# Gated linear attention and a cosine-gated feed-forward on one core: inputs of three batches loaded whole, four state updates dropped, another order

## The chip, the cores and the metric

The kernel runs on one core of a Trainium2 chip. The metric is the device time of one execution, in microseconds (us). Of the kernel before, two timed runs are shown, 201.43 and 202.99, with a median of 202.21. A third execution was recorded by the hardware profiler; its own time is 200.76, and from its first to its last instruction (the span) it took 198.7.

The core has five instruction streams that run side by side. TensorE (PE, with its weight loads as PEld) multiplies matrices and transposes. VectorE (DVE) and ScalarE (ACT) empty PE's results. GpSimd (POOL) prepares operands. SyncE (SP) issues all DMAs here. Each stream does its instructions in the order in which they were written, and waits for what it needs from the others.

## The reference

Per batch (4) and head (8), a gated recurrence runs over 768 positions with rows of 48 numbers. Its output, with the heads side by side, goes through a feed-forward layer of 384 to 2048 to 384.

```python
for t in range(S):                                   # B, H, S, D = 4, 8, 768, 48
    state = alpha[:, :, t, :, None] * state + einsum('bhd,bhe->bhde', k[:, :, t], v[:, :, t])
    y[:, :, t] = einsum('bhd,bhde->bhe', q[:, :, t], state)
x = y.transpose(0, 2, 1, 3).reshape(B * S, H * D)    # 3072 x 384
h = x @ w_in                                         # 384 x 2048
out = (h * cos(h)) @ w_out                           # 2048 x 384
```

The state starts at zero in each batch.

## The kernel before

The 768 positions of a batch are cut into six chunks of 128, so there are 24 chunks, numbered 0 to 23; chunks 0, 6, 12 and 18 are the first of their batch. All work on a chunk is cut into units, each a few instructions, and one long string (ORDER, lines 373 to 401) names the units in the order in which they are to be written into the instruction streams. A unit is a letter with a chunk's number. The scheduling is by hand: the string alone decides in which order each engine does its work.

Loading and preparing a chunk:

- `a`, `k`, `q`, `v` load one chunk's rows of alpha, k, q and v (192 KB each, lines 94 to 103). The rows of eight heads lie far apart in memory, and each row of 48 floats is 192 bytes long. `a` has four buffers of two chunks; the others have six of one chunk each.
- `l` (or `i` for one chunk) takes the logarithm of two chunks' alpha on ACT (line 142). `C` (or `c`) sums it along the positions on PE (lines 155, 159). `E` (or `d`) makes the cumulated product and its inverse with two exponentials on ACT (lines 173, 175).
- `K` and `Q` scale k and q by them on POOL (lines 183, 189; `Q` of chunks 0 and 1 on DVE). `b` casts v to bf16 on POOL (line 193). `E_` makes the mask with which the state is scaled (line 198).

The recurrence within a chunk:

- `T` transposes k and q (line 211, eight transposes), and `t` copies them out on DVE.
- `A` forms the scores (line 228), and `m` masks them on DVE (line 237).
- `S` is the chunk's addition to the state (line 250, four matmuls), and `u` adds and scales the state (line 262 on DVE, line 264 on POOL). The state after the last chunk of a batch is read by nobody, yet it is computed.
- `Y` forms the output (lines 279, 282), `y` casts it (line 289), `D` transposes it (line 298), and `B` copies that out on DVE (line 303).

The feed-forward of a chunk, in two halves:

- `F` and `G` multiply by w_in (line 315, 24 matmuls each). `f_` and `g_` take the cosine on ACT (line 323), and `p` and `Q_` multiply by it on DVE (line 329).
- `V` and `W` multiply by w_out (line 337, eight matmuls each). `e` copies the result out on ACT and stores it (lines 342, 343).

The weights are loaded in four quarters each, 768 KB per DMA: `z0` to `z3` for w_in, `Z0` to `Z3` for w_out (lines 109, 122). They are cast to bf16 by `r` on DVE and `s` on ACT for w_in, and by `R` for w_out (even quarters on DVE, odd quarters on ACT). The float32 copies have tiles of their own, w1f and w2f, so a load never waits for a cast. `F` needs quarters 0 and 1 of w_in, `G` needs 2 and 3; `V` needs quarters 0 and 1 of w_out, and `W` needs 2 and 3.

`w` followed by a number writes that many matmuls on zeros (line 353). Their result is not used; they keep PE occupied. The string holds 69 of them, all written ahead of `F2`.

PE's results lie in three kinds of buffers: "big" (three buffers: `C`/`c`, `A`, `F`, `G` take turns), "g" (one buffer: `T`, `S`, `Y` and `D` take turns, each after the one before has been copied out), and "o" (one buffer, `V` and `W`). DMAs have eight semaphores in turn, so that each DMA is issued only after the one eight before it has landed; SP issues them in the string's order, stores among them.

Of the kernel before, what the change touches and what calls it, by code (L numbers as in the profile page):

```python
# [9 lines left out]
FP = mybir.dt.float32  # L10
# [6 lines left out]
def kernel(  # L17
# [17 lines left out]
    NF = DF // C  # L35
    HF = NF // 2
    HD = H * D
    CW = HD + NP
    ACOL = [(h % 2) * NP + h // 2 for h in range(H)]
    PF = 6  # L40

    consts = ctx.enter_context(tc.tile_pool(name="consts", bufs=1))
    apool = ctx.enter_context(tc.tile_pool(name="apool", bufs=4))
    inpool = ctx.enter_context(tc.tile_pool(name="inpool", bufs=PF))
    cpool = ctx.enter_context(tc.tile_pool(name="cpool", bufs=4))
    work = ctx.enter_context(tc.tile_pool(name="work", bufs=2))
    moe = ctx.enter_context(tc.tile_pool(name="moe", bufs=2))
    ps = ctx.enter_context(tc.tile_pool(name="ps", bufs=1, space=bass.MemoryType.PSUM))
# [31 lines left out]
    nc.vector.memset(m2[0:64, 0:1], 1.0)  # L80
    nc.vector.memset(m2[64:128, 1:2], 1.0)

    w1f = consts.tile([C, 3, DF], FP, tag="w1f")
    w1 = consts.tile([C, 3, DF], BF, tag="w1")
    w2f = consts.tile([C, NF, DM], FP, tag="w2f")
    w2 = consts.tile([C, NF, DM], BF, tag="w2")

    a_t, q_t, k_t, v_t, cp_t, icp_t = {}, {}, {}, {}, {}, {}

    def rows(t, j):  # L90
        b, c = j // NC, j % NC
        return t[b, :, c * C : (c + 1) * C, :].rearrange("h s d -> s h d")

    def load_a(j):
        if j % 2 == 0:
            a_new = apool.tile([C, 2, H, D], FP, tag="a_sb")
            a_t[j // 2] = a_new
        nc.sync.dma_start(out=a_t[j // 2][:, j % 2], in_=rows(alpha, j))  # L98

    def load(nm, src, d, j):  # L100
        t = inpool.tile([C, H, D], FP, tag=nm)
        nc.sync.dma_start(out=t, in_=rows(src, j))  # L102
        d[j] = t

    QF = DF // 4

    def load_w1(h):
        f = slice(h * QF, (h + 1) * QF)
        nc.sync.dma_start(out=w1f[:, :, f], in_=moe_w_in[:, f].rearrange("(k p) f -> p k f", p=C))

    def cast(eng, dst, src):
        if eng is nc.scalar:
# [3 lines left out]

    def cast_w1(h, eng, k0, k1):
        f = slice(h * QF, (h + 1) * QF)
        cast(eng, w1[:, k0:k1, f], w1f[:, k0:k1, f])

    def load_w2(h):
        nc.sync.dma_start(
            out=w2f[:, 4 * h : 4 * h + 4],
            in_=moe_w_out[4 * h * C : (4 * h + 4) * C, :].rearrange("(f p) n -> p f n", p=C),
        )

    def cast_w2(h):
        cast((nc.vector, nc.scalar)[h % 2], w2[:, 4 * h : 4 * h + 4], w2f[:, 4 * h : 4 * h + 4])


    table = [None]
# [6 lines left out]
    def ln(j0, n):  # L138
        lnset()
        g = j0 // 2  # L140
        lo = j0 % 2
        nc.scalar.activation(  # L142
            out=lnab[:, g % 2, lo : lo + n, :, 0:D], in_=a_t[g][:, lo : lo + n], func=AF.Ln
        )

    cum_ps = {}
# [33 lines left out]

    def khat(j):
        icp = icp_t[j // 2][:, j % 2]
        nc.gpsimd.tensor_tensor(out=khb[:, j % 3, :, 0:D], in0=k_t.pop(j),  # L183
                                in1=icp.rearrange("s (h d) -> s h d", h=H), op=ALU.mult)

    def qhat(j):
        cp = cp_t[j // 2][:, j % 2]
        eng = nc.vector if j < 2 else nc.gpsimd
        eng.tensor_tensor(out=qhb[:, j % 3, :, 0:D], in0=q_t.pop(j),  # L189
                          in1=cp[:, 0:HD].rearrange("s (h d) -> s h d", h=H), op=ALU.mult)  # L190

    def vcast(j):
        nc.gpsimd.tensor_copy(out=vpb[:, j % 3, :, 0:D], in_=v_t.pop(j))  # L193

    def emask(j):
        cp = cp_t[j // 2][:, j % 2]
# [46 lines left out]

    U_ps = {}

    def state(j):
        t = ps.tile([C, 512], FP, tag="g")
        U_ps[j] = t
        for p in range(NP):
            nc.tensor.matmul(  # L250
                t[:, p * 96 : (p + 1) * 96],
                khb[:, j % 3, 2 * p : 2 * p + 2].rearrange("s h d -> s (h d)"),
                vpb[:, j % 3, 2 * p : 2 * p + 2, 0:D], start=True, stop=True,
            )

    def ev_state(j):

        t = U_ps.pop(j)[:, 0 : NP * 96].rearrange("r (p e) -> r p e", p=NP)
        sc = t
        if j % NC != 0:  # L260
            sc = work.tile([C, NP, 96], FP, tag="sc")
            nc.vector.tensor_tensor(out=sc, in0=t, in1=ub[:, (j - 1) % 3, :, 0:96], op=ALU.add)  # L262
        eng = nc.vector if j % NC == 0 else nc.gpsimd
        eng.tensor_tensor(  # L264
            out=ub[:, j % 3, :, 0:96].rearrange("r p (a e) -> r p a e", a=2),
            in0=sc.rearrange("r p (a e) -> r p a e", a=2),
            in1=Em_t.pop(j).unsqueeze(3).to_broadcast([C, NP, 2, D]), op=ALU.mult,
        )
# [3 lines left out]
    def outputs(j):  # L272
        t = ps.tile([C, 512], FP, tag="g")
        y_ps[j] = t
        first = j % NC == 0
        qT = qkT_t[j]
        for p in range(NP):
            if not first:
                nc.tensor.matmul(t[:, p * 96 : (p + 1) * 96], qT[:, (NP + p) * C : (NP + p + 1) * C],  # L279
                                 ub[:, (j - 1) % 3, p], start=True, stop=False, skip_group_check=True)  # L280
            for h in (2 * p, 2 * p + 1):
                nc.tensor.matmul(t[:, h * D : (h + 1) * D], A_t[j][:, ACOL[h] * C : (ACOL[h] + 1) * C],  # L282
                                 vpb[:, j % 3, h], start=first, stop=True, skip_group_check=True)
# [63 lines left out]
    def warmup(n):  # L347
# [7 lines left out]

    dve, act_e = nc.vector, nc.scalar
    units = {
        "a": load_a, "k": lambda j: load("k_sb", k, k_t, j), "q": lambda j: load("q_sb", q, q_t, j),
        "v": lambda j: load("v_sb", v, v_t, j), "z": load_w1, "Z": load_w2,
        "r": lambda h: cast_w1(h, dve, 0, 2), "s": lambda h: cast_w1(h, act_e, 2, 3), "R": cast_w2,  # L360

        "i": lambda j: ln(j, 1), "c": lambda j: cums(j, 1), "d": lambda j: exps(j, 1),
# [8 lines left out]
    }  # L371

    ORDER = (
        "a0 i0 q0 q1 a1 c0 v0 d0 Q0 i1 w11 c1 d1 k0 k1 K0 w9 T0 t0 K1 a2 a3 w4 A0 v1 Q1 w1 T1 t1 b0 m0 w9 Y0 "
        "E_0 y0 A1 w2 S0 l1 C1 E1 b1 u0 q2 w1 S1 a4 a5 k2 Q2 v2 k3 E_1 E_2 l2 w9 C2 m1 E2 u1 K2 a6 a7 Y1 y1 "
        "w3 D0 b2 B0 w2 D1 B1 K3 q3 w2 S2 l3 u2 w3 T2 t2 w4 A2 Q3 T3 C3 t3 q4 Q4 m2 k4 K4 E3 w4 T4 t4 z0 s0 "
        "A3 w2 A4 z1 r1 v3 Y2 r0 s1 w1 F0 m3 m4 E_3 E_4 E_5 z2 z3 y2 F1 b3 r2 D2 B2 f_0 p0 f_1 s2 w2 S3 F2 s3 "
        "q5 u3 r3 Q5 p1 Y3 G0 G1 v4 b4 f_2 k5 y3 K5 D3 p2 B3 G2 g_0 Q_0 g_1 g_2 Z1 Z0 Y4 F3 Q_1 y4 R0 Z2 D4 "
        "G3 B4 R1 V0 f_3 T5 Q_2 F4 p3 Z3 g_3 R3 k6 K6 q6 t5 Q6 v5 v6 b5 A5 a8 S4 f_4 R2 E_6 W0 m5 a9 a10 u4 "
        "a11 b6 T6 t6 Q_3 e0 V1 W1 e1 Y5 q7 A6 l4 k7 l5 p4 y5 Q7 V2 m6 S5 K7 u5 W2 e2 q8 D5 B5 k8 k9 C4 E4 Q8 "  # L380
        "C5 S6 v7 V3 u6 Y6 y6 G4 T7 t7 K8 E5 g_4 Q_4 q9 v8 v9 F5 W3 A7 K9 q10 f_5 e3 q11 b7 b8 a12 a13 T8 p5 "
        "b9 t8 G5 m7 D6 B6 V4 g_5 E_7 Q_5 v10 a14 a15 k10 A8 S7 u7 Q9 Q10 E_8 F6 a16 k11 E_9 Y7 y7 v11 G6 m8 "
        "Q11 D7 B7 W4 S8 k12 f_6 p6 F7 u8 g_6 Q_6 E_10 T9 e4 t9 f_7 E_11 V5 l6 l7 S9 u9 p7 W5 e5 q12 q13 Y8 "
        "b10 y8 G7 K10 K11 g_7 D8 B8 A9 m9 C6 E6 T10 t10 Q_7 b11 v12 V6 a17 T11 t11 W6 e6 S10 u10 k13 k14 A10 "
        "Q12 A11 C7 m10 Y9 Q13 y9 V7 q14 m11 D9 F8 E7 l8 B9 Y10 y10 F9 v13 b12 D10 a18 W7 E_12 E_13 B10 f_8 "
        "q15 p8 v14 v15 K12 K13 S11 u11 f_9 p9 K14 q16 F10 f_10 T12 G8 g_8 t12 S12 u12 q17 k15 G9 p10 Y11 e7 "
        "k16 V8 y11 Q_8 D11 B11 a19 g_9 G10 g_10 Q_9 T13 t13 W8 C8 Q_10 K15 A12 b13 S13 Q14 e8 Q15 u13 m12 V9 "
        "T14 b14 t14 l9 W9 Y12 E8 A13 k17 E_14 k18 k19 e9 A14 a20 y12 m13 G11 Y13 y13 F11 m14 D12 B12 E_15 "
        "v16 E_16 g_11 V10 b15 Q_11 S14 u14 a21 a22 a23 f_11 K16 p11 W10 e10 T15 C9 V11 t15 D13 B13 A15 l10 "
        "F12 m15 S15 u15 E9 W11 Y14 k20 y14 f_12 p12 Q16 F13 T16 t16 G12 e11 Y15 y15 b16 v17 V12 v18 f_13 p13 "  # L390
        "E_17 D14 B14 g_12 Q_12 G13 k21 K17 D15 F14 B15 g_13 f_14 q18 q19 q20 Q17 Q_13 S16 u16 b17 W12 e12 "
        "v19 b18 A16 p14 T17 G14 G15 m16 t17 Y16 V13 y16 g_14 Q18 S17 W13 Q_14 g_15 Q_15 K18 u17 C10 E10 A17 "
        "e13 D16 B16 F15 K19 m17 S18 G16 E_18 u18 f_15 Y17 y17 K20 p15 F16 b19 q21 q22 q23 T18 t18 V14 g_16 "
        "f_16 Q19 Q20 Q21 T19 t19 W14 l11 E_19 T20 v20 Q_16 t20 C11 K21 p16 e14 V15 D17 A18 A19 E11 A20 W15 "
        "e15 B17 m18 m19 Q22 S19 u19 G17 g_17 Y18 V16 y18 D18 k22 m20 W16 B18 Y19 v21 y19 Q_17 e16 F17 T21 "
        "t21 K22 v22 v23 f_17 p17 F18 E_20 b20 S20 k23 Q23 u20 G18 f_18 g_18 D19 B19 p18 V17 E_21 E_22 A21 "
        "Y20 y20 Q_18 W17 D20 B20 m21 F19 G19 b21 Y21 e17 F20 f_19 f_20 g_19 y21 D21 V18 K23 p19 B21 p20 W18 "
        "e18 T22 t22 G20 g_20 S21 V19 Q_19 u21 T23 W19 e19 Q_20 A22 t23 A23 m22 b22 S22 u22 F21 f_21 G21 Y22 "
        "y22 m23 V20 g_21 D22 B22 p21 W20 b23 Y23 y23 e20 G22 g_22 Q_21 Q_22 D23 B23 F22 f_22 V21 W21 e21 F23 "
        "G23 p22 V22 W22 f_23 p23 g_23 Q_23 V23 W23 e22 e23 S23 E_23 u23 "  # L400
    )
    for u in ORDER.split():
        nm = u.rstrip("0123456789")
# [29 lines left out]
```

## Time and profile before

| | |
|---|---|
| timed runs, median | 201.43 and 202.99, 202.21 us |
| the profiled execution | 200.76 us, its span 198.7 us |
| PE busy | 189.0 us, 95% of the span |
| DVE, ACT, POOL busy | 139.9, 117.5, 78.5 us |
| DMA, share of 16 engines' span | 72.6% for inputs, weights and stores; 30.27 MB |
| one `F` or `G` (24 matmuls of line 315) | 1.34 us in the chain |
| one `V` or `W` (8 matmuls of line 337) | 1.30 us in the chain |
| matmuls of line 353 (zeros) recorded | 64 of the 69, 18.6 us |
| one load of 192 KB, issue to landing | 4.1 to 4.5 us |
| one weight quarter of 768 KB, issue to landing | 8.3 and 8.7 us |

The profile has one trap. PE's matmuls overlap each other in its records, and the matmuls on zeros count as busy, so "95% busy" does not say how much of the span was useful. A better measure is used below: the time that PE would need for its useful matmuls alone, back to back, against the time at which it reached them.

### The profile page before, as it was taken

To read this page: it belongs to the slowest core of one execution; us is meant where nothing else is said; L and a number is where in the kernel's file an instruction comes from. 1 tells how busy PE (TensorE), PEld (TensorE's weight loads), DVE (VectorE), ACT (ScalarE), POOL (GpSimd) and SP (SyncE) were. 2 spreads that over 40 slices of the span, in tenths; PEclk is the share of its full clock that TensorE was granted. 3 is DMA by queue.
4 is the path that set the end of the run, shared out by engine and by line. 5 is a ranking of instruction groups with operands and counts; after the bars stand their busy time and mean duration, and the time that the engine had idled before them with its cause. 6 is when DMAs were issued, how large, how long until landed. Compare 5 with 4: busy or idle time off the path is not lost.

```text
span 198.7 us, 5949 instructions
## 1 busy us (share of the span) xinstructions
PE 189.0 (95%) x2544; PEld 146.1 (74%) x2549; DVE 139.9 (70%) x186; ACT 117.5 (59%) x133; POOL 78.5 (39%) x124
## 2 busy tenths in 40 slices
PE   1999998999999999999999999999999999999993
PEld 0355456897568687778878779888867978787772
DVE  6137368989754988876887956878597886759541
ACT  3233546786399447986758597467955535433450
POOL 3150881420725684565264128075922440130001
PEclk9999999999999999999999999999999999999999
DMA  6999999999988999999969945930915431111012
GB/s 129 188 186 189 168 338 353 201 379 246 193 196 169 208 175 170 240 217 177 179 145 192 177 99 113 170 79 3 196 45 120 99 66 41 43 40 42 1 43 79
DMA packets 107034, 30.27 MB, mean 152 GB/s; under 512 B 100352, under 2 KB 105472, under 8 KB 107008
## 3 DMA queue, kind: packets, MB, share of 16 engines
q1 hardware_dynamic: 107008, 29.89, 72.6%
q8 instruction: 20, 0.33, 0.8%
q14 instruction: 6, 0.05, 0.1%
HBM read 25.17 MB, written 4.72 MB: 150 GB/s over the span
## 4 chain that ended last, share of the span: by engine, by line
PE 66%; DMA 13%; SPq 11%; DVE 4%; POOL 3%; issue 2%; POOLq 0%; ACT 0%; DVEq 0%
PE o_new L337 26%; PE t L315 25%; DMA t<-in_k_dram 7%; SPq L102 7%; PE t L211 4%; DMA w1f<-in_moe_w_in_dram 4%; SPq L98 4%; PE t L228 2%; PE t L250 2%; PE t L282 2%; DMA t<-in_q_dram 2%; PE t L298 2%; DVE g_new L329 1%; PE t L279 1%; POOL khb L183 1%
## 5 line engine op out<-in xcount | busy, mean ns | idle before, releaser
L315 PE MATMUL t<-x,w 128*128 128x128 bf16 x1152 | 71.2, 219 | 0.9 <-DVE w L115 0.9
L323 ACT ACTIVATE c_sb<-t,halfpi 128x1024 bf16<-128x1024 f32 x48 | 53.0, 1112 | 31.3 <-PE t L315 31.0
L337 PE MATMUL o_new<-w,g_new 128*128 128x384 bf16 x384 | 69.4, 326 | 0.1
L315 PEld LDWEIGHTS <-w 128*128 128x128 bf16 x1152 | 65.5, 98 | 1.6 <-DVE w L115 1.2
L329 DVE TENSOR_TENSOR g_new<-t,c_sb 128x1024 bf16<-128x1024 f32 x48 | 58.0, 1216 | 6.2 <-ACT c_sb L323 6.0
L337 PEld LDWEIGHTS <-g_new 128*128 128x128 bf16 x384 | 35.3, 98 | 20.0 <-issue 0.5
L264 POOL TENSOR_TENSOR ub<-sc,Em 128x384 bf16<-128x384 f32 x20 | 16.9, 844 | 70.4 <-DVE sc L262 70.4
L183 POOL TENSOR_TENSOR khb<-t,icp_new 128x384 bf16<-128x384 f32 x24 | 23.9, 1000 | 25.1 <-DMA t<-in_k_dram 24.5
L237 DVE TENSOR_TENSOR t<-t,mask_f 128x1024 bf16<-128x1024 f32 x24 | 29.0, 1216 | 0.6 <-PE t L228 0.6
L189 POOL TENSOR_TENSOR qhb<-t,cp_new 128x384 bf16<-128x384 f32 x22 | 21.8, 1002 | 16.1 <-ACT cp_new L175 9.2
L217 DVE COPY t<-t 128x1024 bf16<-128x1024 bf16 x24 | 16.5, 688 | 13.4 <-PE t L211 13.1
L289 DVE CAST t<-t 128x384 bf16<-128x384 f32 x24 | 13.3, 556 | 17.0 <-PE t L282 16.9
L342 ACT ACTIVATE o_sb<-o_new 128x384 f32<-128x384 f32 x24 | 11.7, 489 | 22.8 <-PE o_new L337 22.4
L173 ACT ACTIVATE icp_new<-cum_new 128x768 f32<-128x768 f32 (+1 forms) x13 | 9.9, 759 | 15.5 <-PE cum_new L159 15.5
L353 PE MATMUL w_new<-warm 128*128 128x512 bf16 x64 | 18.6, 422 | 0.3 <-issue 0.2
L262 DVE TENSOR_TENSOR sc<-t,ub 128x384 f32<-128x384 f32 x20 | 11.0, 552 | 7.3 <-PE t L250 6.7
L193 POOL CAST vpb<-t 128x384 bf16<-128x384 f32 x24 | 12.5, 522 | 6.2 <-DMA t<-in_v_dram 6.1
L142 ACT ACTIVATE lnab<-a_new 128x768 bf16<-128x768 f32 (+1 forms) x13 | 10.1, 792 | 4.9 <-DMA a_new<-in_alpha_dram 4.9
L303 DVE COPY x<-t 128x384 bf16<-128x384 bf16 x24 | 8.4, 351 | 6.5 <-PE t L298 6.5
L155 PE MATMUL cum_new<-lnab,triu_bf 128*128 128x384 bf16 x24 | 7.3, 334 | 4.3 <-ACT lnab L142 4.3
L282 PE MATMUL t<-vpb,t 128*128 128x48 bf16 x192 | 11.3, 183 | 0.0
L353 PEld LDWEIGHTS <-warm 128*128 128x128 bf16 x69 | 6.4, 104 | 6.2 <-issue 2.5
(46 smaller groups left out, 167.0 us busy)
## 6 DMA issues: line engine op xcount, KB each, us to landing
a_new<-in_alpha_dram SPq DMA_DIRECT2D x24, 192.0 KB, 4.5
t<-in_q_dram SPq DMA_DIRECT2D x24, 192.0 KB, 4.3
t<-in_v_dram SPq DMA_DIRECT2D x24, 192.0 KB, 4.4
t<-in_k_dram SPq DMA_DIRECT2D x24, 192.0 KB, 4.1
out_dram<-o_sb SPq DMA_DIRECT2D x24, 192.0 KB, 2.1
w1f<-in_moe_w_in_dram SPq DMA_DIRECT2D x4, 768.0 KB, 8.3
w2f<-in_moe_w_out_dram SPq DMA_DIRECT2D x4, 768.0 KB, 8.7
```

Of the source, the lines that this page charges most:

```text
L102: nc.sync.dma_start(out=t, in_=rows(src, j))
L183: nc.gpsimd.tensor_tensor(out=khb[:, j % 3, :, 0:D], in0=k_t.pop(j), in1=icp.rearrange("s (h d) -> s h d", h=H), op=ALU.mult)
L189: eng.tensor_tensor(out=qhb[:, j % 3, :, 0:D], in0=q_t.pop(j), in1=cp[:, 0:HD].rearrange("s (h d) -> s h d", h=H), op=ALU.mult)
L217: nc.vector.tensor_copy(out=t, in_=qkT_ps.pop(j))
L237: nc.vector.tensor_tensor(out=t.rearrange("s (h t) -> s h t", h=H), in0=A_ps.pop(j).rearrange("s (h t) -> s h t", h=H), in1=mask_f.unsquee ...
L264: eng.tensor_tensor(out=ub[:, j % 3, :, 0:96].rearrange("r p (a e) -> r p a e", a=2), in0=sc.rearrange("r p (a e) -> r p a e", a=2), in1=E ...
L282: nc.tensor.matmul(t[:, h * D : (h + 1) * D], A_t[j][:, ACOL[h] * C : (ACOL[h] + 1) * C], vpb[:, j % 3, h], start=first, stop=True, skip_g ...
L315: nc.tensor.matmul(t[:, f], w1[:, kk, ft * C : (ft + 1) * C], x_t[j][:, kk], start=(kk == 0), stop=(kk == 2))
L323: nc.scalar.activation(out=c_sb, in_=h_ps[j, half], func=AF.Sin, bias=halfpi, scale=1.0)
L329: nc.vector.tensor_tensor(out=g_new, in0=h_ps.pop((j, half)), in1=c_t.pop((j, half)), op=ALU.mult)
L337: nc.tensor.matmul(o_ps[j][:, 0:DM], g[:, f], w2[:, half * HF + f], start=(f == 0 and half == 0), stop=(f == HF - 1 and half == 1))
L353: nc.tensor.matmul(w_ps, warm[:, 0:C], warm, start=True, stop=True)
```

## The change

- Batch 0 is still loaded chunk by chunk. Of batches 1 to 3, alpha, k, q and v are each loaded by one DMA of 1152 KB, at the first chunk's load unit: 4 x 3 = 12 large loads in place of 72 small ones. In the built program such a DMA reads four neighbouring rows at once (768 bytes) and writes them as four pieces of 192 bytes into four partitions: its source has the shape 32 x 48 x 192 floats, its destination is given by a shape register as 32 x 48 x 4 x 48.
- Each input has two buffers of a whole batch. k's rows lie 64 floats apart there instead of 48.
- The float32 weights share four buffers of a quarter each. The quarter `Z1` takes the buffer of `z0`, `Z0` that of `z1`, `Z2` that of `z2`, `Z3` that of `z3`; so each load of w_out waits for the casts of a quarter of w_in.
- `S`, `E_` and `u` of chunks 5, 11, 17 and 23 are left out. The state's three slots are counted without these chunks.
- The pool of the exponentials has three buffers of two chunks instead of four.
- ORDER is another string. It holds 82 matmuls on zeros instead of 69.

```diff
+    PAD = {"a": 48, "k": 64, "q": 48, "v": 48}
...
-    apool = ctx.enter_context(tc.tile_pool(name="apool", bufs=4))
-    inpool = ctx.enter_context(tc.tile_pool(name="inpool", bufs=PF))
-    cpool = ctx.enter_context(tc.tile_pool(name="cpool", bufs=4))
+    inpool = ctx.enter_context(tc.tile_pool(name="inpool", bufs=2))
+    cpool = ctx.enter_context(tc.tile_pool(name="cpool", bufs=3))
...
+    def load(nm, src, j):
         b, c = j // NC, j % NC
-        return t[b, :, c * C : (c + 1) * C, :].rearrange("h s d -> s h d")
...
+        if c == 0:
+            t_new = inpool.tile([C, H, NC, PAD[nm]], FP, tag=nm)
+            in_t[nm, b] = t_new
+        t = in_t[nm, b]
+        if b == 0:
+            nc.sync.dma_start(out=t[:, :, c, 0:D],
+                              in_=src[b, :, c * C : (c + 1) * C, :].rearrange("h s d -> s h d"))
+        else:
+            nc.sync.dma_start(out=t.rearrange("p h c d -> p (h c) d")[:, :, 0:D],
+                              in_=src[b].rearrange("h (c p) d -> p (h c) d", p=C))
...
     def load_w1(h):
         f = slice(h * QF, (h + 1) * QF)
-        nc.sync.dma_start(out=w1f[:, :, f], in_=moe_w_in[:, f].rearrange("(k p) f -> p k f", p=C))
+        t = inpool.tile([C, 3, QF], FP, tag="wf", bufs=4)
+        nc.sync.dma_start(out=t, in_=moe_w_in[:, f].rearrange("(k p) f -> p k f", p=C))
+        wf_t[h] = t
...
+    def us(j):
+        return (j // NC * (NC - 1) + j % NC) % 3
```

The beginnings of the two orders, up to the first `W`; first before, then after:

```diff
-a0 i0 q0 q1 a1 c0 v0 d0 Q0 i1 w11 c1 d1 k0 k1 K0 w9 T0 t0 K1 a2 a3 w4 A0 v1 Q1 w1 T1 t1 b0 m0 w9 Y0
-E_0 y0 A1 w2 S0 l1 C1 E1 b1 u0 q2 w1 S1 a4 a5 k2 Q2 v2 k3 E_1 E_2 l2 w9 C2 m1 E2 u1 K2 a6 a7 Y1 y1
-w3 D0 b2 B0 w2 D1 B1 K3 q3 w2 S2 l3 u2 w3 T2 t2 w4 A2 Q3 T3 C3 t3 q4 Q4 m2 k4 K4 E3 w4 T4 t4 z0 s0
-A3 w2 A4 z1 r1 v3 Y2 r0 s1 w1 F0 m3 m4 E_3 E_4 E_5 z2 z3 y2 F1 b3 r2 D2 B2 f_0 p0 f_1 s2 w2 S3 F2 s3
-q5 u3 r3 Q5 p1 Y3 G0 G1 v4 b4 f_2 k5 y3 K5 D3 p2 B3 G2 g_0 Q_0 g_1 g_2 Z1 Z0 Y4 F3 Q_1 y4 R0 Z2 D4
-G3 B4 R1 V0 f_3 T5 Q_2 F4 p3 Z3 g_3 R3 k6 K6 q6 t5 Q6 v5 v6 b5 A5 a8 S4 f_4 R2 E_6 W0
+v0 b0 a0 a1 q0 i0 c0 q1 v1 v2 d0 Q0 k0 k1 i1 w7 c1 E_0 K0 k2 a2 a3 a4 d1 Q1 a5 w18 T0 b1 k3 t0 w4 S0
+A0 u0 q2 m0 w7 Y0 q3 l1 y0 b2 C1 K1 w1 T1 t1 w4 D0 A1 B0 E1 K2 l2 K3 w1 S1 Q2 E_1 u1 w3 T2 t2 C2 z0
+w1 A2 m1 m2 w2 Y1 E_2 E_3 z1 z2 s1 y1 s2 z3 Q3 w5 T3 t3 w4 A3 s0 v3 D1 B1 q4 v4 r1 m3 b3 r0 k4 k5 E2
+Q4 w2 S2 u2 w11 Y2 r2 q5 F0 f_0 F1 r3 y2 D2 s3 p0 f_1 G0 G1 a6 Z1 B2 g_0 g_1 p1 Q_0 K4 T4 t4 K5 F2
+f_2 Z0 Q5 Q_1 A4 m4 T5 b4 t5 w9 A5 p2 l3 l4 Y3 y3 R1 m5 w1 C3 E3 Z2 D3 B3 C4 E4 w2 S3 Z3 G2 g_2 u3
+E_4 S4 u4 R0 R3 k6 G3 q6 Y4 y4 F3 K6 v5 v6 K7 D4 R2 E_6 f_3 V0 B4 Q_2 g_3 Q_3 W0
```

After it the new string goes on with `a12 F4 Q6 Q7 e0 b5 V1 W1 p3 e1 f_4 p4 Q8 K8 G4 g_4 V2 T6 E_7 E_8 Q9 t6 Q_4 T7 t7 W2 Y5 b6 y5 D5 B5 A6 A7 T8 t8 l5 b7 m6 G5 e2 q12 b8 g_5 S6 u6 V3 S7 l6 K9 W3 e3 u7 T9 m7 C5 E5 t9 C6`. In the new string SP's loads come in this order: 17 of 192 KB (v0 first, then a0, a1), the four quarters of w_in, six of 192 KB, alpha of batch 1, the four quarters of w_out, k and q of batch 1, v5, v of batch 1, alpha of batch 2, and then the rest between the stores.

## The prediction, made before the changed kernel was run

> **What bounds the kernel now.** I read the strip of 40 slices first (busy tenths, granted clock, DMA), each slice 5 us.
>
> ```profile
> PE   1999998999999999999999999999999999999993
> PEclk9999999999999999999999999999999999999999
> DMA  6999999999988999999969945930915431111012
> GB/s 129 188 186 189 168 338 353 201 379 246 193 196 169 208 175 170 240 217 177 179 145 192 177 99 113 170 79 3 196 45 120 99 66 41 43 40 42 1 43 79
> ```
>
> PE is busy and its clock granted from start to end; DMA is full for two thirds of the span. Which of them binds, and where? The chain that ended last says it: DMA issues and landings until about 64 us, then PE alone.
>
> ```profile
> 15.13 0.99 SPq L102
> 16.17 0.96 SPq L98
> ...
> 23.11 7.49 DMA w1f<-in_moe_w_in_dram
> ...
> 38.63 10.57 DMA t<-in_k_dram
> ...
> 66.30 1.34 PE t L315 x24
> ...
> 190.15 5.21 PE o_new L337 x32
> 195.39 0.50 ACT o_sb L342
> ```
>
> From it I take PE's useful work. Per chunk: `F`+`G` 2 x 1.34, `V`+`W` 2 x 1.30 (5.21/4), `T` 0.45, `A` 0.33, `S` 0.17, `D` 0.17, and from PE's timeline `Y` 0.38 (0.20 in a batch's first chunk) and the sums 0.27: 7.05 us. Times 24, less 4 x 0.18, is 168.5; without `S23`, which comes last, 168.3. The last `W` ends at 190.15 + 5.21 = 195.4. So PE lost 195.4 - 168.3 = 27.1 us before that, and a tail of 3.3 follows: 27.1 + 168.3 + 3.3 = 198.7, the span. Counting the units written before two points shows when it was lost: before `F0` (starts 31.98) stand 7.9 us of work, so 24.1 were lost by then; before `W0` (starts 49.18) 23.6, so 25.6. What held `W0` is seen in two rows of the timelines of ACT and PE:
>
> ```profile
> 48.52 1.48 ACT L113 ACTIVATE w<-w2f 128x1536 bf16<-128x1536 f32 x1 [1.95 <-DMA w2f<-in_moe_w_out_dram]
> ...
> 49.18 1.68 PE L337 MATMUL o_new<-w,g_new 128*128 128x384 bf16 x8
> ```
>
> (The first row is the cast of the last quarter of w_out; `W0` takes 1.68 instead of 1.30, as its second half waits for it.) So only the loss of the first 65 us can change; the rest is PE back to back.
>
> **The dropped states.** Four `S`: 4 x 0.17 = 0.7 us less of PE, all work 167.8. Their `u` and `E_` lie on DVE and POOL beside PE. At the end `S23` and `u23` fall away, but the store of the last result, issued at 195.90, is as late as they are (median landing 2.1 us): tail unchanged, at most 0.2 gained.
>
> **More matmuls on zeros.** One takes 0.21 us (9 in 2.10 us), in the first 5 us of PE's work 0.43 (11 in 4.85). They stand in PE's order, so nothing passes them. After: v0 is loaded ahead of a0, so alpha lands one load later and PE starts at about 5.6 instead of 4.3. Then 82, of which 10 slow: 4.3 + 72 x 0.21 = 19.4. So at least 25.0 us are lost whatever the loads do; the span can't fall below 25.0 + 167.8 + 3.3 = 196.1, that is 1.3% under 198.7. In before the same sum is 4.3 + 4.7 + 12.2 = 21.2 of 27.1.
>
> **The price of a whole batch, B.** Not in this trace. Bounds: 192 KB loads follow each other every 1.04 us (chain), and 1152 KB at the 188 GB/s of those slices is 6.3 us; at the 353 to 379 GB/s of the weight slices 3.1 to 3.3. The reads become 768 bytes, between the 192 of inputs and the 1536 to 2048 of weights; the writes stay 192. Over 16 engines 188 GB/s is 16.3 ns for 192 bytes, and 379 is 65 ns for 1536: a line through them gives 37 ns for 768, so B = 96 x 37 = 3.6 us if reads decide and about 6.3 if writes do. I take 3.6 to 4.2, since only the weight rows, which are long on both sides, are known to be fast, and the input rows are scattered on the reading side; and keep 3.1 to 6.3. Less than 3.1, or a shape register that issues more slowly than that, nothing in the rows shows.
>
> [...]
>
> **The opening, step by step**, with durations of the trace (192 KB every 1.04, w_in quarters 2.1, w_out quarters 2.6, as from the landing of the load ahead at 38.1 to the last quarter's at 48.5, POOL products 1.0, DVE masks and gates 1.2). PE: `c0` 5.6; `w7`, `c1`, `w18` until 14.0; `T0` 14.0, `A0` 15.5, `w7`, `Y0` 17.5, `T1` 18.4, `A1` 20.0, `T2` 22.1 (waits 0.8 for `Q2` on POOL), `A2` 23.5, `Y1` 24.8 (masks), `w5`, `T3` 26.2, `A3` 27.6, `w11`, `Y2` 31.1. The w_in quarters land from 23.8 to 30.5, four loads earlier than before, but `r1`, `m3`, `r0` on DVE end at 31.2: `F0` at 31.5. Work before it is 6.5, lost 25.0 (before 24.1).
>
> `F0` to `G1` end at 37.4. `T4` to `A5` go at DVE's pace (`p0`, `p1`, `Q_0`, `t4`, `Q_1`, `m4`, `t5` fill it until 42.2), with `w9` (1.9) in that wait. Then `C3`, which before came after `W0`: its buffer is `F2`'s, free after `p2` at 43.4; ACT has the logarithms by then (table load 1.28, 2 x 0.84) if alpha of batch 1 has landed, at 36.0 + B = 39.6 to 40.2. ACT goes on with `R1` (the cast, 1.48), `E3` and `E4` (1.5 each), another table load and `g_2` until 50.1, then `R3` until 51.6. PE beside it: `D3`, `C4`, `w2`, `S3`, `G2`, `S4`, `G3`, `Y4`, `F3`, `D4`, `V0` end at 51.9. The last w_out quarter lands at 36.0 + B + 10.4 = 50.0 to 50.6, and its cast waits for ACT about as long. `W0` starts at 51.9 after 22.8 us of work: 29.1 lost, 3.5 more than before. Behind the casts on ACT stand the cosines that free the buffers of `F3` and `F4`; they fit.
>
> After `W0`, k and q of batch 1 land 2B after the last quarter, at 57.2 to 59.0, `Q6` on POOL about 1.1 later; `T6` is reached 7.9 us after `W0`, at 59.8. So nothing waits, or hardly; before, this stretch lost 1.5 (to 27.1), after I take 0.5: 29.6. A load of 1152 KB ahead of a store delays it by B; the result tiles have three buffers and a chunk takes 7 us: hidden; uncovered it would cost B once.
>
> Sum: 29.6 + 167.8 + 3.3 = 200.7, 2.0 over the span of 198.7. The profiled execution took 200.76, 2.06 over its span; the median is 202.21, 1.45 above that. Forecast 202.21 + 2.0 = 204.2.
>
> **Rivals.**
> (1) The opening fits better than my count, bubbles filled by the matmuls on zeros as laid out: 26.5 lost by `W0`, 27.0 in all: 198.1, 201.6. For it: the floor is 25.0. Against: DVE was busy 9.4 of 10 us between 30 and 50 us, and `C3` with ACT's work is now ahead of `W0`.
> (2) Slower by over 2%: the 192-byte writes set the price, B = 6.3. The last quarter lands at 52.7, `W0` ends 0.8 later; k and q follow at 65.3, `Q6` 66.4, against 60.5 for `T6`: 5.9 more. Alpha of batch 2 lands after four large loads, at 79; ACT's `l6` waits, and with it `C6`, which PE reaches at 76: another 3 to 4. In all +2.0 + 0.8 + 5.9 + 3.5 = 12.2: 214.4. For it: the writes don't change. It decides from where 2B + 1.1 after the last quarter passes `T6`: B about 4.8; the 2% are reached at about 5.1.
> (3) Large loads don't come as one stream (the shape register slows the issue): B over 6.3, 215 to 225. No row speaks for it.
> (4) The change does nothing for the time: lost 27.1 again, 0.7 saved: 201.5. It is inside the first rival's reach.
>
> **How the numbers follow.** Forecast (B under 4.8): 0.60, with its own range 201.8 to 207, as some 40 hops between engines, 0.04 to 0.09 us of "issue" each in the chain, are not in my count; of it 0.14 lies above 206.3. Rivals (1) and (4) together 0.10, of which 0.03 under 198.2 (below the floor's 199.6 only by the scatter of the runs). Rival (2), B from 4.8 to 6.3: 0.24, of which 0.22 over 206.3. Rival (3) 0.06. Two per cent is about what a measurement of this kernel can tell. Faster 0.03; slower 0.14 + 0.22 + 0.06 = 0.42; within 0.55. Range 201.3 to 212: below it half of (1) and (4), above it (3) and the end of (2).
>
> **What would show it.** The large loads' issue to landing and the GB/s of their slices (over 280: reads decide; under 200: writes). `F0` at 31.5, line 142's two logarithms of chunks 6 to 9 ahead of the w_out casts on ACT, `W0` near 52, line 211's `T6` near 60 without a POOL wait ahead of it. From 65 us on PE back to back. I'm wrong if `W0` starts before 50, if PE waits in the second half, or if line 183 or 189 waits for DMA past 60 us.

## The result and the profile after

| | before | after |
|---|---|---|
| timed runs | 201.43 and 202.99, median 202.21 us | 226.26 and 228.41, median 227.33 us |
| ratio after to before, 95% interval | | 1.124 [1.095, 1.154] |
| profiled execution, its span | 200.76, 198.7 us | 226.26, 224.4 us |
| mean granted clock of TensorE | 1.00 | 0.954 |
| DMA packets | 107034 | 50778 |

The kernel is slower by 12%, 25 us. That is outside the forecast's range (201.3 to 212), in the direction to which the forecast gave 0.42.

The strip of 40 slices of the changed kernel (5.6 us each), to be read beside the first one of before:

```profile
PE   0999999778927899999069999999999999999993
...
PEclk9999999999995599999659999999999999999999
DMA  8999999999999999999980006919201010110111
GB/s 127 182 173 236 375 214 180 212 366 225 170 185 177 198 237 195 168 201 179 205 136 32 17 26 131 153 37 178 73 35 38 35 38 4 70 38 3 37 38 70
DMA packets 50778, 30.27 MB, mean 135 GB/s; under 512 B 25664, under 2 KB 49216, under 8 KB 50752
```

There are two holes in PE's row (slices 12 and 20), and each is followed by a stretch at half clock (0.50 for 10.24 us), which before had none. The packets are half as many, and yet the DMA engines are full for as long as before, at 168 to 237 GB/s from 56 to 112 us: reading four rows at once has not made the stream faster.

The chain that ended last, in order of time, shows what PE waited for in the two holes (start, us, what):

```profile
45.60 21.01 DMA t_new<-in_q_dram
66.68 1.00 POOL qhb L190
67.73 0.62 PE t L212 x4
...
70.14 2.56 PE o_new L341 x8
...
97.04 2.81 SPq L347
...
100.07 10.01 DMA t_new<-in_k_dram
...
112.44 0.95 POOL khb L184
113.39 0.46 POOL vpb L194
113.89 0.48 PE t L254 x4
```

First hole: q of batch 1 lands 21 us after its issue, `Q6` follows on POOL, and the second half of `T6`, the transposes of q, starts at 67.73, where PE had been ready at 63.04. Second hole: k of batch 2 is issued at 100.07 only and lands 10 us later; POOL then works through `K12`, `u10`, `K13` and `b12` in its order, and `S12`, which needs `K12` and `b12`, starts at 113.89 where PE had been ready at 106.56. The row at 112.44 is `K13`. (v, which `b12` casts, had landed at 101.89; the cast stood in line behind `K12`.) The row at 70.14 shows the half clock: eight matmuls of line 341 take 2.56 us instead of 1.30.

The same stretches by engine, after and before (start:end, length, then busy us and count of PE, PEld, DVE, ACT, POOL, then granted clock, DMA share, GB/s). After:

```profile
62.00:82.00 20.00, 13.88 (x130) 10.30 (x128) 8.50 (x12) 8.03 (x9) 9.65 (x15) 0.74 0.99 197
82.00:105.00 23.00, 22.84 (x371) 19.68 (x370) 19.17 (x26) 14.45 (x17) 9.03 (x12) 1.00 0.99 191
105.00:121.00 16.00, 8.67 (x76) 5.68 (x74) 4.31 (x7) 5.97 (x8) 7.15 (x13) 0.68 0.72 136
```

Before:

```profile
62.00:82.00 20.00, 19.92 (x298) 16.34 (x296) 15.44 (x20) 13.59 (x15) 12.79 (x20) 1.00 1.07 189
82.00:105.00 23.00, 23.00 (x335) 18.80 (x333) 18.49 (x25) 16.58 (x19) 11.77 (x17) 1.00 0.99 191
105.00:121.00 16.00, 16.00 (x234) 12.93 (x233) 11.65 (x16) 12.62 (x15) 5.73 (x11) 1.00 0.68 137
```

The last two numbers of each row are what matters. From 62 to 121 us the DMAs of both kernels are equally full and move the same bytes per second. Before, PE doesn't notice; after, it stands still for 12 us. So the same stream delivers the same bytes in another order: not the rows of the next chunks, but whole tensors, of which five sixths are for later.

Counted as in the prediction, useful work that PE had lost by each time:

| by (us) | before | after | what lies between |
|---|---|---|---|
| 31.5 | 23.6 | 24.9 | opening, up to `F0` |
| 63.0 | 26.3 | 32.1 | `C3` waits for alpha 1.5, `G3` for an exponential 1.3, `W0` for the cast 0.6 |
| 67.7 | 26.5 | 36.8 | first hole, 4.7 |
| 78.0 | 26.6 | 42.5 | half clock (67.6 to 77.9), 5.7 |
| 106.5 | 26.8 | 42.9 | |
| 113.9 | 26.8 | 50.3 | second hole, 7.4 |
| 119.0 | 26.8 | 52.6 | half clock (108.6 to 118.8), 2.3 |

After that PE is dense again: its record is busy for 99.1 of the 99.1 us from 121.0 to 220.1.

### The profile page after: what moved, and what is told of

The parts are those of the page before. It is cut to its first block, busy times and chain, and to the rows that moved or that the text cites. A ratio compares the mean times of both kernels' runs of the same rounds, so it can differ in the third digit from the quotient of the medians.

```text
span 224.4 us, 5824 instructions
## 1 busy us (share of the span) xinstructions
PE 197.1 (88%) x2541; PEld 151.2 (67%) x2546; DVE 138.8 (62%) x182; ACT 116.5 (52%) x133; POOL 74.2 (33%) x116
## 2 busy tenths in 40 slices
DMA packets 50778, 30.27 MB, mean 135 GB/s; under 512 B 25664, under 2 KB 49216, under 8 KB 50752
## 4 chain that ended last, share of the span: by engine, by line
PE 69%; DMA 16%; DVE 5%; SPq 2%; POOL 2%; issue 2%; ACT 1%; DVEq 0%; POOLq 0%; ACTq 0%
PE o_new L341 24%; PE t L319 23%; DMA t_new<-in_q_dram 9%; PE w_new L357 5%; PE t L212 5%; DMA t_new<-in_k_dram 4%; PE t L229 3%; PE t L286 2%; PE t L302 2%; PE cum_new L156 2%; DMA t_new<-in_alpha_dram 2%; DVE g_new L333 2%; PE t L283 2%; SPq L347 1%; PE t L254 1%
## 5 line engine op out<-in xcount | busy, mean ns | idle before, releaser
L341 PE MATMUL o_new<-w,g_new 128*128 128x384 bf16 x384 | 71.5, 334 | 0.8 <-ACT w L113 0.6
L327 ACT ACTIVATE c_sb<-t,halfpi 128x1024 bf16<-128x1024 f32 x48 | 52.8, 1113 | 36.8 <-PE t L319 33.4
L184 POOL TENSOR_TENSOR khb<-t_new,icp_new 128x384 bf16<-128x384 f32 x24 | 23.8, 1001 | 34.1 <-DMA t_new<-in_k_dram 15.0
L190 POOL TENSOR_TENSOR qhb<-t_new,cp_new 128x384 bf16<-128x384 f32 x22 | 21.8, 1000 | 20.5 <-ACT cp_new L176 13.9
L346 ACT ACTIVATE o_sb<-o_new 128x384 f32<-128x384 f32 x24 | 11.8, 491 | 31.5 <-PE o_new L341 31.5
L268 POOL TENSOR_TENSOR ub<-sc,Em 128x384 bf16<-128x384 f32 x16 | 13.3, 831 | 39.6 <-DVE sc L266 39.4
L357 PE MATMUL w_new<-warm 128*128 128x512 bf16 x77 | 20.9, 402 | 0.4 <-issue 0.2
L194 POOL CAST vpb<-t_new 128x384 bf16<-128x384 f32 x24 | 12.2, 519 | 22.1 <-DMA t_new<-in_v_dram 12.1
L142 ACT ACTIVATE lnab<-t_new 128x768 bf16<-128x768 f32 (+1 forms) x13 | 10.2, 796 | 17.4 <-DMA t_new<-in_alpha_dram 10.6
L266 DVE TENSOR_TENSOR sc<-t,ub 128x384 f32<-128x384 f32 x16 | 8.9, 556 | 9.4 <-PE t L254 6.3
L212 PE MATMUL t<-ident_bf,qhb 128*128 128x128 bf16 x96 | 10.2, 235 | 4.9 <-POOL qhb L190 4.9
L254 PE MATMUL t<-vpb,khb 128*128 128x96 bf16 x80 | 6.8, 209 | 7.3 <-POOL vpb L194 7.3
```

The source lines that it names most:

```text
L184: nc.gpsimd.tensor_tensor(out=khb[:, j % 3, :, 0:D], in0=inp("k", j), in1=icp.rearrange("s (h d) -> s h d", h=H), op=ALU.mult)
L190: eng.tensor_tensor(out=qhb[:, j % 3, :, 0:D], in0=inp("q", j), in1=cp[:, 0:HD].rearrange("s (h d) -> s h d", h=H), op=ALU.mult)
L212: nc.tensor.transpose(t[:, (i * NP + p) * C : (i * NP + p + 1) * C], src[:, j % 3, 2 * p : 2 * p + 2].rearrange("s h d -> s (h d)"), ident_bf)
L268: eng.tensor_tensor(out=ub[:, us(j), :, 0:96].rearrange("r p (a e) -> r p a e", a=2), in0=sc.rearrange("r p (a e) -> r p a e", a=2), in1=E ...
L327: nc.scalar.activation(out=c_sb, in_=h_ps[j, half], func=AF.Sin, bias=halfpi, scale=1.0)
L341: nc.tensor.matmul(o_ps[j][:, 0:DM], g[:, f], w2[:, half * HF + f], start=(f == 0 and half == 0), stop=(f == HF - 1 and half == 1))
```

## The experiments

Each is one execution, except the last, which was timed in three rounds. Beside them, on the same chip, the kernel before took 201.6 to 202.2 us (on one of the chips it ran 13 times, from 200.91 to 202.89), so a difference of 2 us or less between single executions says nothing. Gains are counted from the profiled 226.26 us. "Lost" is the count of the table above, at the end of the run unless a time is given; the changed kernel has 52.8 by it, the kernel before 26.9.

**Long pieces on the writing side.** The large loads keep place, bytes and 768-byte reads, but each 768 bytes go to one partition. The rows of k also lose their padding (48 floats instead of 64); those of q, v and alpha had none.

```diff
-            nc.sync.dma_start(out=t.rearrange("p h c d -> p (h c) d")[:, :, 0:D],
-                              in_=src[b].rearrange("h (c p) d -> p (h c) d", p=C))
+            nc.sync.dma_start(out=t.rearrange("p h c d -> p (h c d)").rearrange("p (n e) -> p n e", e=4 * D),
+                              in_=src[b].rearrange("h s d -> (h s d)").rearrange("(n p e) -> p n e", p=C, e=4 * D))
```

> The twelve large loads keep their place, their 1152 KB and their 768-byte reads, but write 768 bytes into one partition instead of four pieces of 192 into four (k's rows without padding). The rows then stand in other partitions, so the output is computed from permuted inputs; the amount of work is the same. Theory W (the 192-byte writes set the price of a large load): a large load's stream falls from the 6.1 to 6.6 us seen to about 3.6, the waits of POOL for q at 63 us and for k at 101 us disappear, the granted clock stays at 1.0, and the time is what the blind count gave for B = 3.6, 202 to 207 us. Theory R (768-byte reads, or large loads as such, are slow here): 6 us and 225 to 230 again. Theory O (the new order is bad whatever the loads cost): loads quicken, but the time stays over 215.

Measured 204.37 us, span 202.6, full clock throughout. Its strip:

```profile
PEclk9999999999999999999999999999999999999999
DMA  7999999999999689710811261460111101111012
GB/s 119 188 183 193 339 333 169 319 371 350 311 313 308 213 235 333 213 42 31 240 46 39 69 209 39 110 205 3 39 42 39 42 5 39 42 39 42 2 42 78
```

From 51 to 66 us the large loads now run at 308 to 313 GB/s, and from 66 us on the DMAs have gaps. When the loads landed (us), from the DMA records of both traces:

| | k batch 1 | q 1 | v 1 | alpha 2 | q 2 | alpha 3 | v 2 | k 2 |
|---|---|---|---|---|---|---|---|---|
| after | 60.55 | 66.62 | 73.86 | 80.03 | 88.19 | 95.67 | 101.89 | 110.08 |
| long pieces | 53.33 | 56.90 | 61.24 | 65.19 | 70.72 | 77.42 | 80.98 | 86.39 |

Loads that follow each other directly are 6.1 to 6.2 us apart in the changed kernel (k 1 to q 1, v 1 to alpha 2, alpha 3 to v 2), and 3.6, 4.0 and 3.6 here. Packets of 768 bytes take 69 ns in the median there and 36 ns here; packets of 192 bytes in either kernel's small loads take 18 to 20. So a 768-byte read that is written as four pieces costs about as much as four reads of 192. The padding has no part in it: the loads of q and v, which never had any, quicken too. With long writes and all else as in the changed kernel, the order of loads included, neither hole is there, and 22 of the 25 us are gone.

**Pieces of 384 bytes.** This kernel was to exclude another reading: that the price comes from the form of the load (a shape register, one read spread over four partitions).

```diff
-            nc.sync.dma_start(out=t.rearrange("p h c d -> p (h c d)").rearrange("p (n e) -> p n e", e=4 * D),
-                              in_=src[b].rearrange("h s d -> (h s d)").rearrange("(n p e) -> p n e", p=C, e=4 * D))
+            nc.sync.dma_start(out=t.rearrange("p h c d -> p (h c d)").rearrange("p (n e) -> p n e", e=2 * D),
+                              in_=src[b].rearrange("h s d -> (h s d)").rearrange("(n p e) -> p n e", p=C, e=2 * D))
```

> As e1_long_writes, but each large load writes pieces of 384 bytes (two rows) into one partition instead of 768; place, bytes and order the same, inputs permuted within a batch. If the length of the written piece sets the price: a 384-byte piece costs between the 17 ns of a 192-byte piece and the 36 ns of a 768-byte one. At about 24 ns a large load takes about 4.5 us (192 pieces in each of 16 engines) and the kernel 204 to 208. If any piece under 768 bytes costs as much as four rows of 192 do (34 ns for 384 bytes): 6.5 us a load and 222 to 228. If instead the price of the changed kernel came from the form of its load (a shape register, four partitions from one read) and not from the length of the pieces: as e1, 203 to 206, with 18 ns or less for 384 bytes.

Measured 205.06 us, span 203.3. The load has the form of the changed kernel's: the packets are reads of 1536 bytes, each written as four pieces into four partitions; the pieces are twice as long. Loads land 4.5 us apart (54.49 to 59.03, 81.39 to 85.87); one pair, v 1 to alpha 2, lies 5.4 apart (64.03 to 69.46), while the stream goes on at 253 GB/s, against the 262 of 4.5 us. The large loads are in slices 11 to 18 (5.1 us each):

```profile
GB/s 120 188 183 197 351 316 183 286 373 321 249 247 269 250 284 255 255 192 8 210 98 40 67 207 42 85 225 7 39 42 39 42 5 39 42 39 41 2 42 77
```

A large load has 384, 192 or 96 pieces per DMA engine when the pieces are 192, 384 or 768 bytes, so a piece costs 16.1 ns (6.2 us / 384), 23.4 ns (4.5 / 192) or 37.5 ns (3.6 / 96). That is close to 9 ns and 7.2 ns for each 192 bytes. The form of the load is not what costs; the length of the written piece is. The reads are longer here too, 1536 bytes instead of 768; that reads don't count while the pieces are 192 bytes is shown below, by six loads with 192-byte reads that take 6.1 us as well. And 4.5 us lies under the 4.8 that the forecast gave as the point from which the wait of `T6` decides: PE has no hole over 0.9 us after 20 us.

**The old order with the large loads.** The order of before, with the first chunk's load unit standing for the batch, and the four states dropped.

```diff
-a6 a7 a8 a9 ... k6 k7 q6 q7 ... S5 ... E_5 ... u5
+a6 ... k6 q6 ...
```

> The order of compute of before, with the twelve large loads at the place of each batch's first load unit, the shared weight buffers, and without the four states. Theory G: slower than before by 10 to 30 us (212 to 232), with POOL waiting for DMA past 60 us and the clock granted at 0.5 after a long wait. Theory O: 200 to 204.

Measured 227.52 us, span 224.8, clock 0.947. PE's holes are from 56.5 to 62.2, 62.8 to 68.2 and 113.1 to 117.6, and one of 3.0 us at 26.4:

```profile
PE   1999678999018999999929999999989999999993
...
PEclk9999958999755999999997999999999999999999
```

So the large loads cost the old order as much as the new one. The new order of the other units is not needed for the 25 us: with the large loads, either order gives 227.

**The new order with small loads, by tensor.** Each large load becomes its six loads of 192 KB, at the same place.

```diff
-a6 ... k6 ... q6
+a6 a7 a8 a9 a10 a11 ... k6 k7 k8 k9 k10 k11 ... q6 q7 q8 q9 q10 q11
```

> Each large load replaced by six loads of 192 KB at the same place, so the order of the bytes in the queue is that of after; only the reads are 192 instead of 768 bytes, and each chunk's part lands by itself. Theory W: six small loads take 6.2 to 6.6 us like one large one, so the reading of four rows at once gains nothing; Q6 can start some 5 us and K12 some 5 us earlier than after, and the time is 213 to 221. If reading four rows does gain, six small loads take clearly longer than the large one and the time is not under 222. If only the order of tensors mattered and not the landing by parts, 225 to 229.

Measured 219.12 us, span 217.2, lost 45.9. The six small loads of q of batch 1 take 6.1 us (from 61.07, where the last of k landed, to 67.14), as much as the one large load. So the wide reads gain nothing, and landing by parts is worth 7 us: `T6` no longer waits for chunk 11's rows. Other holes are left, the longest 3.0 us (from 46.7) and 3.7 us (from 78.4).

**The new order with small loads, sorted by use.** Three versions. In the first, I set the loads out by hand:

> The new order of compute, the same tiles, but batches 1 to 3 are loaded by 72 loads of 192 KB, in the order in which the chunks are used (k, q, v of a chunk together). Bytes and price per byte are those of before. Theory G (at an unchanged price, what costs is that a chunk waits for whole tensors of a batch): the stalls at 63 and 107 us disappear and the time is 203 to 209. Theory O (the order of compute): over 215.

Measured 234.31 us: a failed experiment. Alpha stood too late in my list, and ACT, which takes the logarithms in order, held PE from 72.0 to 78.1 us (alpha of chunks 12 and 13), from 89.9 to 102.8 (chunks 16 and 17) and from 147.3 to 151.1 (chunks 22 and 23). ACT's row in the longest of these holes:

```profile
97.59 0.84 ACT L138 ACTIVATE lnab<-t_new 128x768 bf16<-128x768 f32 x1 [8.14 <-DMA t_new<-in_alpha_dram]
```

In the second, every load stands 45 units ahead of its first user, except the first eleven of batch 1 (12 to 43):

> As e2_need_order, but the 192 KB loads of batches 1 to 3 now stand in the order in which the new order of compute first uses them (in e2 two chunks of alpha that ACT's row of logarithms needs early stood behind 20 other loads), each some 45 units ahead of its use. Theory G: no wait of POOL for DMA over 3 us past 60 us, clock 1.0, 203 to 209. If the order of compute itself can't be fed at 190 GB/s: over 212.

Measured 212.40 us, span 210.6. It stayed close to the long pieces up to 80 us (31.7 lost against 30.5), then had one hole, from 81.08 to 86.52. ACT's timeline has its cause (start, us, line, operation, and the idle time ahead of it):

```profile
81.34 0.84 ACT L138 ACTIVATE lnab<-t_new 128x768 bf16<-128x768 f32 x1 [4.17 <-DMA t_new<-in_alpha_dram]
```

The logarithm of chunks 16 and 17 waits for alpha, and the cosines that free PE's buffers stand behind it on ACT. In the third, alpha's loads of chunks 10 to 23 stand 75 units ahead (58 for chunks 10 and 11, 69 for 12 and 13); nothing else is changed:

> As e2b_use_order (small loads sorted by first use, 45 units ahead, the changed order of the other units), but alpha's loads of batches 2 and 3 and of chunks 10, 11 stand 75 units ahead instead of 45, the rest unchanged in order. If the one wait for alpha of chunks 16 and 17 (gap of PE from 81.1 to 86.5 us, then 6.8 us at half clock) was all that kept e2b from the long-write kernel's 204.4: 203 to 207, with no gap over 2 us after 65 us and full clock throughout. If the price of the changed order lies elsewhere and that wait only showed where it lay: another load (k, q or v of batches 1 and 2) becomes the late one, 208 to 214, with a new gap between 60 and 110 us, since the queue carries the same bytes at the same rate.

Measured 205.82 us, span 203.9, full clock, no hole over 0.9 us after 35 us. Its DMA row is as full as that of the changed kernel up to 92 us, at much the same rate:

```profile
DMA  7999999999999999997899264369531501110012
GB/s 117 189 171 180 345 344 161 173 366 313 166 195 185 232 155 224 179 190 162 168 188 202 70 111 107 91 117 193 119 79 42 116 3 42 42 40 19 22 42 77
```

So 20 us of the 25 are got back by the same bytes at the same speed, when they come in parts and in the order in which they are used. The rest, 3.9 us over before, arises ahead of 72 us: 29.1 lost by 55 us against 26.4 before, and 32.0 by 72 us against 26.7.

**No half clock.** Useless matmuls fill both holes: the transposes of k in `T6` are done 21 times, and 32 matmuls on zeros stand ahead of the four of `S10`.

```diff
-            for p in range(NP):
+            for p in tuple(range(NP)) * (1 + FILL_T.get((j, i), 0)):   # 20 for chunk 6, k
...
+        for _ in range(FILL_S.get(j, 0)):                              # 32 for chunk 10
+            nc.tensor.matmul(t, warm[:, 0:C], warm, start=True, stop=True)
```

> After, with PE kept at work in its two long waits: the four transposes of k in T6 are issued 21 times over (they write the same values), and 32 matmuls on zeros stand in S10 ahead of its own four. The loads are those of after. If the idle PE lowered the clock: it is granted 1.0 throughout, and the time falls by 4 to 9 us (218 to 223), as the stretches at 0.5 hold about 10 us of PE's work each, part of which then waits for loads. If the clock has another cause: 0.5 again, and 226 to 230.

Measured 224.49 us, span 222.6. Its clock, over 40 slices:

```profile
PEclk9999999996999988999999999999999999999998
```

After the filled holes the clock stays full; it falls twice elsewhere, for 3.4 us each, after gaps of 1.9 and 2.1 us. Only 1.8 us of the span are gained, less than expected and within the scatter of single executions, though the half clock had stood against 8.0 of the lost us. The reason is in the landings: k of batch 2 lands at 110.52 (110.08 in the changed kernel), and `S12` starts at 114.33 instead of 113.89. The 5.7 us that PE had lost at half clock ahead of that, it loses here on useless matmuls and other waits; only the 2.3 us behind the last hole could be gained. PE's slowness had been cover for the loads. So the half clock is mostly a consequence here and not a second price on top.

**The place of k of batch 2.** In the order of loads, k of batch 2 stands behind alpha of batch 3 and v of batch 2. Two kernels move it: directly behind q of batch 2, or in exchange with alpha of batch 3.

```diff
-q12 ... a18 ... v12 ... k12
+q12 k12 ... a18 ... v12
```

> After, with the load of k of batch 2 moved in the string from before W5 to just behind the load of q of that batch, so ahead of alpha of batch 3 and v of batch 2 in SP's queue; nothing else changes. If the wait at 107 us is k12's place in the queue (POOL waits for k, u10 and v's cast queue behind it): that wait and the second stretch at 0.5 disappear, 216 to 220. If it is bandwidth alone (the next load is late instead): 223 to 228.

```diff
-q12 ... a18 ... v12 ... k12
+q12 ... v12 k12 ... a18
```

> The changed kernel, with alpha of batch 3 and k of batch 2 exchanged in the order of loads (q12, v12, k12 and then a18, where k12 stood); all else as it is. If the second gap (106.6 to 113.9 us, then 2.3 us lost at half clock) comes from the place of k of batch 2 behind a load that nobody needs yet: k lands near 100, the gap and its half clock go, 9 to 10 us less than the changed kernel's 226.3: 216 to 218, with the first gap (63 to 67.7 us) as it was. If the stream of loads is too slow in any order: the gap stays or moves to alpha of batch 3 (line 142), 221 to 226.

Measured 222.13 and 221.02 us (spans 220.4 and 219.2): they gain 4.1 and 5.2 us, the first between its two expectations, the second at the edge of the slow one, and the second hole is still 5 us long (104.98 to 109.96, for v landing at 109.35; 104.55 to 109.58, for k landing at 105.77 and POOL's work behind it). `S12` starts 3.9 and 4.3 us sooner than at 113.89. The place is about half of what that hole and its half clock cost, 9.7 us. How the loads are issued may have a part in the other half. SP's timeline of the exchanged kernel (start, us, line):

```profile
78.44 0.71 SPq L97 DMA_DIRECT2D t_new<-in_q_dram  x1
80.62 6.76 SPq L347 DMA_DIRECT2D out_dram<-o_sb  x1
87.60 0.71 SPq L97 DMA_DIRECT2D t_new<-in_v_dram  x1
```

With a large load ahead of it, a store of 192 KB takes 6.76 us to be issued, where one with none ahead takes 0.33 (the changed kernel at 122.10); only then does SP come to the next load. From 85 to 90 us the DMA engines are half idle in that kernel:

```profile
85.00:90.00 5.00, 5.00 (x99) 4.90 (x96) 4.88 (x7) 3.76 (x4) 2.48 (x6) 1.00 0.48 116
```

No run removes the stores from SP's queue, so how much of the hole that costs stays open.

**The dropped states alone.** The kernel before without `S`, `E_` and `u` of chunks 5, 11, 17 and 23.

```diff
-... S5 ... E_5 ... u5 ... S11 ... E_11 ... u11 ... S17 ... S23 ...
+... (none of them)
```

> The kernel before without S, E_ and u of chunks 5, 11, 17 and 23, whose results nobody reads; nothing else. The blind count gives 4 x 0.17 = 0.7 us less on PE, and up to 0.2 at the end: a ratio of 0.995 to 0.999. If the states filled waits that stay: 1.000.

Measured over three rounds: ratio 0.999, interval [0.996, 1.002], 201.91 against 201.74 us. The 0.7 us of the sum lies inside the interval; it is neither shown nor excluded.

## Why the prediction was wrong

- **What bounds the kernel before: right, but read too narrowly.** "So only the loss of the first 65 us can change; the rest is PE back to back." PE was back to back there because each 192 KB came ahead of its use, from DMAs that were full until 110 us; the old order with large loads (227.52 us) shows how little it took to change that. That they were full stands in the strip that I quoted; I took them to be beside the path, and a change of the loads moves them onto it.
- **The failing step: the price of a whole batch.** "I take 3.6 to 4.2, since only the weight rows, which are long on both sides, are known to be fast." It measured 6.1 to 6.2. The very row that I used for the line through two points had long pieces on both sides and could not tell reads from writes; the input loads, with 192 bytes on both sides, couldn't either. The long-piece kernels told it: 3.6 us with 768-byte pieces, 4.5 with 384, 6.2 with 192. The bound of 6.3 was right, the choice inside the bounds was wrong. By that alone the sum would have given the 214.4 of the second rival; what was still missing stands there, below.
- **The price by the length of the written piece** shows no step between the three lengths: 16.1 ns for 192 bytes, 23.4 for 384 and 37.5 for 768 lie on one line (191 GB/s over 16 engines at the short end, 328 at the long one). Longer reads alone changed nothing that shows: six loads with rows of 192 bytes took 6.1 us, a large one with reads of 768 bytes 6.1 to 6.2.
- **The opening ledger: right up to 40 us, and close after that for its own B.** `F0` was forecast at 31.5 with 25.0 lost; it started at 31.39 with 24.9. With B at 3.6 (the long pieces) `W0` starts at about 50.9, forecast 51.9; `T6` at 59.26, forecast 59.8. That the time is 204.37, forecast 204.2, is partly luck: the span of 202.6 is 1.9 over the sum's 200.7 (31.3 us lost instead of 29.6), and this execution took 1.8 us over its span where the forecast had put 3.5. At the true B `C3` came at 44.31 instead of 43.4, as alpha landed at 43.39 instead of 40, and the last cast ended at 55.0 instead of 51.6. ACT and PE show the end of it (start, us):

```profile
53.50 1.48 ACT L113 ACTIVATE w<-t 128x1536 bf16<-128x1536 f32 x1 [0.62 <-DMA t<-in_moe_w_out_dram]
```

```profile
52.31 2.11 PE L341 MATMUL o_new<-w,g_new 128*128 128x384 bf16 x12
55.03 0.81 PE L341 MATMUL o_new<-w,g_new 128*128 128x384 bf16 x4 [0.61 <-ACT w L113]
```

  This is the pair of rows that was shown of before: the second half of `W0` again waits for the cast of the last quarter, now at 55.0.
- **"A load of 1152 KB ahead of a store delays it by B … hidden": wrong as to who is delayed.** The store's result tile is hidden indeed. But SP issues in order, and the issue itself is held, so the next load is delayed with the store. SP's timeline of the changed kernel:

```profile
94.06 5.80 SPq L347 DMA_DIRECT2D out_dram<-o_sb  x1
100.07 0.70 SPq L97 DMA_DIRECT2D t_new<-in_k_dram  x1
```

- **The second rival: right mechanism, half the price.** It had the writes, the wait of `T6` (5.9 forecast, 4.7 measured) and the point from which it decides. It gave 214.4 against 227.3. Three terms, 17.1 us together, make up more than the difference of 12.9: the second hole at `S12` (7.4 us), which it did not look for, as it followed the loads only as far as alpha of batch 2; the two stretches at half clock (8.0 us together); and an opening that had lost 32.1 by 63 us instead of 29.6 + 0.8 = 30.4. Against them, its wait of `C6` (3.5) did not come, as PE was late by then, and the wait of `T6` was 1.2 shorter.
- **The third rival** named 215 to 225 for a slow issue through the shape register. The time was near, the reason not: large loads with no other load in flight were issued in 1.27 and 0.71 us (k and v of batch 3, at 135.31 and 150.50), and the kernel with 384-byte pieces, which uses the register too, takes 205.06.
- **The dropped states** at 0.7 us, and **the matmuls on zeros** as a floor of 25.0 lost: nothing speaks against either, and nothing shows them. The first is smaller than what three rounds could tell; the second was reached by no kernel, as the least that any kernel in the new order lost in all is 31.3 us, with the long pieces.
- **What was to show it** worked: under 200 GB/s in the large loads meant writes; line 190 waited for a DMA past 60 us; PE waited in the second half.

## What to carry to other kernels

Price a DMA by both of its sides: a read made four times as long gained nothing while it was still written in pieces of 192 bytes (6.1 to 6.2 us for 1152 KB, against 6.1 in short reads). (Short reads written in long pieces were not run.) Where a stream of loads is full, order and grain are part of the critical path even if no engine waits today: one load for a whole batch makes its first chunk wait for its last, and everything behind it in the queue too (here 20 of the 25 us came back with loads in parts, in the order of use). When a change slows a stream, follow it to its last load and not only to the first wait.

## What the hardware showed that was not expected

- Holes in PE's work were followed by half clock, and the length of the hole did not set that of the stretch. In the changed kernel the clock changes at 67.65, 77.89, 108.61 and 118.85 us, all of them whole multiples of 3.41 us apart; over the runs the stretches lasted 3.41, 6.83, 10.24 or 13.65 us. They were 10.24 us with holes of 4.7 and 7.3 us (the changed kernel), 6.8 with one of 5.4 (the first version 45 units ahead), 3.4 with one of 5.0 (the exchanged kernel) and with 1.9 and 2.1 (the filled kernel). With the changed kernel's record of PE cut along these changes into pieces of 3.41 us, the clock fell after pieces with 3.41 us (64.23 to 67.65) and 2.05 us (105.20 to 108.61) idle, and stayed full after one with 1.25 us idle (47.17 to 50.58). Both times it came back after a piece without idle time; after one with 0.65 us idle (71.06 to 74.47) it was still at half. No run shows what decides between these figures.
- SP's issue of a DMA was held for 4 to 13 us while a large load ahead of it was in flight (12.7 us for q of batch 1, issued at 45.60 behind k and four weight quarters). A large load issued late in the one ahead took 0.70 us (k of batch 2 at 100.07, 1.8 us before v landed); with no other load in flight, large loads took 1.27 and 0.71 us and a store 0.33.
